# A hand-written schedule of an attention and expert kernel: when two rounding DMAs, a negation and a copy are issued

## The chip, the cores and the metric

The kernel runs on one core of a Trainium2 chip. The metric is device time in microseconds of one execution; the median of three runs of the kernel before is 603.72 us (603.69 to 610.67). The core has five engines that take their instructions in order and meet through semaphores: TensorE (PE; PEld is its weight load), VectorE (DVE), ScalarE (ACT), GpSimd (POOL) and SyncE (SP). PE, DVE, ACT and POOL compute; SP, ACT and POOL also issue DMAs.

## The reference

Attention with a decay bias for 8 batches of 8 heads (576 positions, width 64), then an expert layer for 128 chosen tokens of each batch:

```
scores = (1/8) * q @ k.T
cum    = cumsum(max(s, 0))
scores = where(causal, -1e9, scores + min(-(cum_i - cum_j), 0))
attn   = softmax(scores);   x = attn @ v          # 64 heads
top    = the 128 tokens of a batch with the highest x @ w_gate
out    = x;  out[top] += sigmoid(x[top] @ w_gate) * (relu(x[top] @ w1) @ w2)
```

## The kernel before

One head n is worked through in some 25 small operations. PE multiplies numbers that are rounded to a shorter format (float32r). So that no accuracy is lost, k and q are each kept as a rounded value and a remainder, in four tiles: KA and QA (five buffers each, line 134) hold the rounded values and a few extra rows, KB and QB (four buffers each) hold the remainders and second copies of the rounded values. These operations (lines 149 to 171) fill them:

- hk(n), hq(n): POOL issues a DMA of k or q of head n from HBM; the DMA rounds on its way into KA or QA ("ka<-in_qk_dram" and "qa<-in_qk_dram" in the views).
- kn(n): ACT writes the negated rounded k into the lower half of KB. ka(n): POOL issues a DMA that adds the exact k onto it ("kb<-in_qk_dram"); what stays is the remainder. kb(n): ACT copies the rounded k into the upper half of KB. kn and kb look alike in the views: ACT "kb<-ka".
- qn(n): ACT writes the negated rounded q into QB (ACT "qb<-qa"). qa(n): POOL's adding DMA onto it ("qb<-in_qk_dram"). qb(n): SP copies the rounded q into the other half of QB ("qb<-qa").

With them, PE makes the scores twice. s0 to s3 (tiles "s") have queries on the partitions and serve only for each row's maximum, which DVE takes ("mj<-s", "m"). mrows(n) turns the five columns of maxima into rows on PE ("s<-ident,m"), ACT negates them ("mr<-s") and issues a small DMA ("qa<-mr") that puts them into QA as one more row of the product. st0 to st3 (tiles "st") have keys on the partitions, from KA, QA and then KB, QB; ACT takes their exponential ("pt<-st"), POOL zeroes the part above the diagonal ("pt<-pt"), and av0 to av3 multiply with v on PE ("pa<-vt,pt"). DVE divides by the sums ("xt<-pa,z") and SP stores. The tiles s and st share four PSUM buffers (psS, line 126): a new one starts when ACT or DVE has read what stood in its buffer.

Work on the experts' weights, the choice of tokens and the experts' products ("w1hl", "sct", "ph", "py") is cut into small steps, of which one follows in each slot.

The order is written out by hand. START (line 44) lists the first operations one by one. After it, time is cut into slots, eight to a head; an operation at position p in SCHEDULE (line 57) is emitted for head n in slot 8n + p, and within a slot in the list's order (line 780). So for the head n whose st0 is in slot 8n, hk(n) stands 32 slots ahead, four heads earlier. InOrder (line 24) keeps every engine's instructions in this order. Nothing here is a time: a slot lasts as long as the engines need.

Of the kernel before, what the change touches and what calls it, by code (L numbers as in the profile page):

```python
# [23 lines left out]
class InOrder:  # L24
# [18 lines left out]

START = [
# [4 lines left out]
    ("rows", 3), ("fill", 5), ("rows", 2), ("fill", 2), ("kn", 2), ("qn", 2), ("qb", 2),  # L49
# [6 lines left out]
]  # L56
SCHEDULE = [
# [5 lines left out]
]  # L63

# [774 lines left out]
```

## Time and profile before

| | |
|---|---|
| median of three runs | 603.72 us (603.69 to 610.67) |
| the profiled execution | 610.3 us; its span, first to last instruction, 608.6 us |
| PE busy | 537.2 us (88%) |
| DVE, ACT, POOL busy | 326.1 (54%), 295.3 (49%), 301.6 us (50%) |
| mean granted clock of TensorE | 0.909 |
| software DMA queue (POOL's) | 42.55 MB, 36.4% of 16 engines' span |

A row of the timeline gives start, duration, engine and operation, and in brackets the idle time of the engine before it and what ended that. A row of the waits gives who waited for whom, the sum, the number of times and the longest. The granted clock (PEclk) is 1.00 at 2.4 GHz and 0.50 at 1.2 GHz; a value between is a mean over a stretch that has both.

### The profile page before, as it was taken

How to read it: one execution, taken by the hardware profiler on the slowest of the kernel's cores; microseconds unless marked ns; L12 is line 12 of the kernel's file. 1: busy time of each engine (PE TensorE's matmuls, PEld its weight loads, DVE VectorE, ACT ScalarE, POOL GpSimd, SP SyncE). 2: the span in 40 equal slices, each digit the busy share in tenths (PEclk: the TensorE clock that was granted, in tenths of full speed). 3: DMA queues.
4: the chain of work that ended last, by engine and by line, in shares of the span. 5: the costliest groups of instructions: out<-in, count | busy, mean ns of one | idle time of the engine just before them, and what ended most of it. 6: DMA issues, size and time to landing. Idle time of an engine off the chain costs nothing. (4 is left out here: it accounts for less than half of the span.)

```text
span 608.6 us, 11656 instructions
## 1 busy us (share of the span) xinstructions
PE 537.2 (88%) x3843; PEld 491.2 (81%) x3843; DVE 326.1 (54%) x1350; ACT 295.3 (49%) x658; POOL 301.6 (50%) x629
## 2 busy tenths in 40 slices
PE   6978877888988799778999989899898898999996
PEld 2767767788877798678999988899788888999874
DVE  6434435655456647366466646565265635573562
ACT  4545355544555455555564445564354455652121
POOL 8554444446555565465554455444455546433240
PEclk8977789978899959898999979999998869999999
DMA  5856766565676775655656766565566666532200
GB/s 129 193 127 133 164 147 164 109 135 121 149 162 129 174 182 126 158 123 122 132 123 141 158 154 129 114 132 95 132 157 135 135 139 133 129 64 40 89 19 34
DMA packets 54798, 78.04 MB, mean 128 GB/s; under 512 B 7705, under 2 KB 26452, under 8 KB 54738
## 3 DMA queue, kind: packets, MB, share of 16 engines
q0 software_dynamic: 22080, 42.55, 36.4%
q1 hardware_dynamic: 29724, 30.38, 18.8%
q10 hardware_dynamic: 2934, 4.36, 2.3%
q8 instruction: 31, 0.51, 0.3%
q14 instruction: 29, 0.24, 0.1%
HBM read 55.84 MB, written 11.53 MB: 111 GB/s over the span
## 5 line engine op out<-in xcount | busy, mean ns | idle before, releaser
L34 PE MATMUL pa<-vt,pt 128*96 128x95 f32 (+2 forms) x1920 | 248.8, 277 | 3.3 <-POOL pt L34 3.3
L34 PEld LDWEIGHTS pa<-vt,pt 128*96 128x96 f32 (+2 forms) x1920 | 235.8, 193 | 8.3 <-POOL pt L34 4.7
L34 POOL TENSOR_SCALAR_AFFINE_SELECT pt<-pt 128x128 f32<-128x128 f32 (+1 forms) x320 | 119.0, 464 | 244.5 <-ACT pt L34 244.0
L34 DVE CUSTOM_DVE_ANT_0 mj<-s,maskf 128x192 bf16<-128x192 f32 (+4 forms) x320 | 140.5, 470 | 120.7 <-PE s L34 118.9
L34 ACT ACTIVATE pt<-st 128x288 f32<-128x288 f32 (+3 forms) x320 | 124.3, 440 | 89.1 <-PE st L34 65.3
L34 PE MATMUL st<-qa,ka 67*128 67x288 f32 (+9 forms) x384 | 128.8, 344 | 24.5 <-ACT pt L34 16.2
L34 PE MATMUL s<-ka,qa 66*128 66x64 f32 (+4 forms) x384 | 120.3, 374 | 28.5 <-ACT mr L34 22.5
L34 ACT ACTIVATE qb<-qa 64x576 fp32r<-64x576 f32 x64 | 43.7, 683 | 146.8 <-DMA qa<-in_qk_dram 146.7
L34 PE MATMUL st<-qb,kb 128*128 128x288 f32 (+4 forms) x384 | 108.4, 317 | 0.0
L34 PEld LDWEIGHTS st<-qa,ka 67*128 67x128 f32 (+3 forms) x384 | 77.6, 202 | 36.7 <-ACT pt L34 22.9
L34 PEld LDWEIGHTS s<-ka,qa 66*128 66x128 f32 x384 | 73.7, 220 | 36.3 <-ACT mr L34 25.9
L34 ACT ACTIVATE kb<-ka 64x576 fp32r<-64x576 f32 x128 | 86.9, 679 | 7.9 <-DMA ka<-in_qk_dram 4.1
L34 PEld LDWEIGHTS st<-qb,kb 128*128 128x128 f32 (+1 forms) x384 | 77.7, 202 | 1.4
L34 POOL DMA_DIRECT2D kb<-in_qk_dram x64 | 71.3, 1114 | 2.5 <-issue 2.2
L34 POOL DMA_DIRECT2D ka<-in_qk_dram x66 | 54.9, 832 | 3.8 <-DMA ka<-in_qk_dram 1.1
L34 POOL DMA_DIRECT2D qa<-in_qk_dram x66 | 53.7, 813 | 3.5 <-issue 2.0
L34 POOL DMA_DIRECT2D qb<-in_qk_dram x64 | 54.3, 848 | 0.0
L34 DVE CUSTOM_DVE_ANT_0 mj<-s,maskf,md 128x64 bf16<-128x64 f32 x64 | 18.0, 281 | 31.7 <-PE s L34 30.5
L34 DVE TENSOR_TENSOR xt<-pa,z 128x320 f32<-128x320 f32 x64 | 31.1, 486 | 0.1
L34 POOL DMA_INDIRECT out_dram<-xe,idx x8 | 8.6, 1070 | 36.6 <-DVE xe L34 26.7
L34 DVE CUSTOM_DVE_ANT_0 junk<-xt,wg 128x512 bf16<-128x512 f32 (+1 forms) x40 | 26.5, 681 | 0.2
L34 DVE DVE_READ_ACCUMULATOR2_ANT m<- 128x1 f32 x320 | 26.4, 83 | 0.0
(284 smaller groups left out, 517.8 us busy)
## 6 DMA issues: line engine op xcount, KB each, us to landing
vt<-in_v_dram SPq DMA_DIRECT2D x32, 325.0 KB
ka<-in_qk_dram POOLq DMA_DIRECT2D x66, 144.0 KB, 3.7
qa<-in_qk_dram POOLq DMA_DIRECT2D x66, 144.0 KB, 4.2
qb<-qa SPq DMA_DIRECT2D x64, 144.0 KB
kb<-in_qk_dram POOLq DMA_DIRECT2D x64, 144.0 KB, 4.4
qb<-in_qk_dram POOLq DMA_DIRECT2D x64, 144.0 KB, 3.4
out_dram<-xt SPq DMA_DIRECT2D x32, 192.0 KB
wr<-in_w_dram ACTq DMA_DIRECT2D x16, 256.0 KB
```

The source lines that it names most:

```text
L34: return self._tc.keep_in_program_order(call(*args, **kwargs))
```

## The change

Six entries of SCHEDULE get other positions, two entries of the list trade places within their slot (kb and qn), and START gets another order. hk moves from 32 to 34 slots ahead of its head's slot 8n and hq from 30 to 33; qn from 26 to 18, kb from 18 to 10, qa from 15 to 11, and qb from 19 to 21. No operation is added or removed, and no buffer changes. In START, hq of head 2 and hk, hq of head 4 move ahead, v of heads 2 and 4 is loaded later, and the fills (matmuls on zeros) between them are dealt out in another way.

```diff
 START = [
     ("vload", 0), ("rows", 0), ("s0", 0), ("s1", 0), ("fill", 2), ("kn", 0), ("qn", 0), ("qb", 0),
-    ("hk", 2), ("ka", 0), ("qa", 0), ("kb", 0), ("s2", 0), ("s3", 0), ("hq", 2), ("kn", 1), ("qn", 1), ("qb", 1),
+    ("hk", 2), ("hq", 2), ("ka", 0), ("qa", 0), ("kb", 0), ("s2", 0), ("s3", 0), ("kn", 1), ("qn", 1), ("qb", 1),
     ("fill", 5), ("kb", 1), ("ka", 1), ("qa", 1), ("rows", 1), ("s0", 1),
-    ("vload", 2), ("hk", 3), ("hq", 3), ("s1", 1), ("mrows", 0), ("s2", 1), ("s3", 1),
+    ("hk", 3), ("hq", 3), ("hk", 4), ("hq", 4), ("s1", 1), ("mrows", 0), ("s2", 1), ("s3", 1),
...
 SCHEDULE = [
-    ("norm2", 16), ("av0", 10), ("s2", -14), ("side", 0), ("norm0", 15), ("hk", -32),
-    ("kb", -18), ("av2", 13), ("kn", -21), ("qb", -19), ("hq", -30), ("ka", -13),
+    ("norm2", 16), ("av0", 10), ("s2", -14), ("side", 0), ("norm0", 15), ("hk", -34),
+    ("qn", -18), ("av2", 13), ("kn", -21), ("qb", -21), ("hq", -33), ("ka", -13),
...
```

On ACT the place is the end of a head's work, between the exponentials of st2 and st3 of head 9 and those of st0 and st1 of head 10. Before (the first "kb<-ka" is kn(12), the second kb(12); "qb<-qa" is qn(13); w1hl is a copy of weights):

```order
L34 ACTIVATE kb_87<-ka_86 64x576
L34 ACTIVATE pt9_1097<-st9_2_1134 128x288
L34 ACTIVATE pt9_1097<-st9_3_1139 128x288
L34 ACTIVATE pt9_1097<-st9_3_1139 96x96
L34 ACTIVATE w1hl_147<-wr6_1057 128x512
L34 ACTIVATE kb_87<-ka_86 64x576
L34 ACTIVATE qb_89<-qa_88 64x576
L34 ACTIVATE mr11_1188<-s11_3_1130 5x128
L34 DMA qa_88<-mr11_1188 1x5x128
L34 ACTIVATE pt10_1195<-st10_0_1196 128x448
```

The same place with the change, from the exponential of st2 on ("qb<-qa" is now qn(12), and "kb<-ka" behind it kb(11)):

```order
L34 ACTIVATE pt9_1095<-st9_2_1131 128x288
L34 ACTIVATE pt9_1095<-st9_3_1136 128x288
L34 ACTIVATE pt9_1095<-st9_3_1136 96x96
L34 ACTIVATE w1hl_147<-wr6_1054 128x512
L34 ACTIVATE qb_89<-qa_88 64x576
L34 ACTIVATE kb_87<-ka_86 64x576
L34 ACTIVATE mr11_1187<-s11_3_1127 5x128
L34 DMA qa_88<-mr11_1187 1x5x128
L34 ACTIVATE pt10_1193<-st10_0_1194 128x448
```

The two operations have changed places, and both now serve one head earlier in the row of heads than they did: the negation stays in the same place of the period and takes the q of another head.

On POOL, head 8's zeroing and the four DMAs of its period, before ("qb" is qa(10), "qa" hq(12), "kb" ka(10), the last "ka" hk(13)):

```order
L34 AFFINE_SELECT pt8_1005<-pt8_1005 128x128 x3
L34 DMA qb_89<-in_qk_dram 64x576
L34 DMA qa_88<-in_qk_dram 64x576
L34 DMA kb_87<-in_qk_dram 64x576
L34 AFFINE_SELECT pt8_1005<-pt8_1005 128x128
L34 AFFINE_SELECT pt8_1005<-pt8_1005 96x96
L34 DMA ka_86<-in_qk_dram 64x576
L34 AFFINE_SELECT pt9_1097<-pt9_1097 128x128 x3
```

And with the change ("kb" is ka(10), "qb" qa(10), "ka" and "qa" hk(13) and hq(13)):

```order
L34 AFFINE_SELECT pt8_1003<-pt8_1003 128x128 x3
L34 DMA kb_87<-in_qk_dram 64x576
L34 AFFINE_SELECT pt8_1003<-pt8_1003 128x128
L34 AFFINE_SELECT pt8_1003<-pt8_1003 96x96
L34 DMA qb_89<-in_qk_dram 64x576
L34 DMA ka_86<-in_qk_dram 64x576
L34 DMA qa_88<-in_qk_dram 64x576
L34 AFFINE_SELECT pt9_1095<-pt9_1095 128x128 x3
```

One DMA instead of three now stands between the two groups of zeroing of a head, and three behind the second; hq is of one head later.

On PE, in head 8, the scores of head 10, with what each waits for; before:

```order
L34 MATMUL pa1_151<-vt6_614,pt7_916 128x95 [waits Pool_49]
L34 MATMUL pa1_151<-vt6_614,pt7_916 128x95 x2
L34 MATMUL s10_2_1023<-ka_86,qa_88 128x512 [waits DVE_49]
L34 MATMUL pa1_151<-vt6_614,pt7_916 128x95 x3
L34 MATMUL s10_3_1035<-ka_86,qa_88 128x64 [waits Activation_49]
L34 MATMUL st8_2_1039<-qa_88,ka_86 128x288 [waits DVE_49]
```

And with the change:

```order
L34 MATMUL pa1_151<-vt6_611,pt7_914 128x95 [waits Pool_49]
L34 MATMUL pa1_151<-vt6_611,pt7_914 128x95 x2
L34 MATMUL s10_2_1020<-ka_86,qa_88 128x512 [waits Activation_49]
L34 MATMUL pa1_151<-vt6_611,pt7_914 128x95 x3
L34 MATMUL s10_3_1032<-ka_86,qa_88 128x64 [waits DVE_49]
L34 MATMUL st8_2_1036<-qa_88,ka_86 128x288 [waits Activation_49]
```

The order of PE's work is the same, but the four PSUM buffers are dealt out in another way: the buffer in which head 9's maxima were turned, which ACT must read as mr(9), goes to s2 of head 10 instead of s3, one group of av matmuls sooner.

## Rows read from the trace of the kernel before

**Rows 1.** Page, part 1: busy us, share of the span, instructions

```profile
PE 537.2 (88%) x3843; PEld 491.2 (81%) x3843; DVE 326.1 (54%) x1350; ACT 295.3 (49%) x658; POOL 301.6 (50%) x629
```

**Rows 2.** Waits of PE over the whole span: us in total, times, longest

```profile
PE s L34 <- ACT mr L34: 22.5, 19, 2.5
PE st L34 <- ACT pt L34: 16.2, 25, 1.1
...
PE st L34 <- DMA qa<-in_qk_dram: 3.8, 1, 3.8
```

**Rows 3.** Waits of ACT over the whole span

```profile
ACT qb L34 <- DMA qa<-in_qk_dram: 146.7, 56, 6.0
```

**Rows 4.** Stretches by stage: length, busy of each engine, clock, DMA share, GB/s

```profile
core 0: us, PE busy (x) PEld busy (x) DVE busy (x) ACT busy (x) POOL busy (x), PEclk, DMA share, GB/s
...
45.25:287.44 242.19, 203.70 (x1434) 188.83 (x1432) 129.97 (x545) 124.06 (x278) 126.75 (x264) 0.87 0.64 143
287.44:346.64 59.20, 59.20 (x475) 56.45 (x474) 35.11 (x153) 31.63 (x73) 29.97 (x63) 1.00 0.63 139
346.64:370.21 23.57, 21.74 (x163) 20.71 (x162) 11.89 (x55) 12.51 (x28) 14.05 (x31) 0.86 0.63 141
370.21:434.02 63.81, 60.84 (x493) 57.69 (x492) 37.51 (x164) 33.25 (x76) 28.77 (x62) 1.00 0.58 127
434.02:508.56 74.54, 65.69 (x468) 61.23 (x467) 38.20 (x169) 37.11 (x84) 39.48 (x87) 0.86 0.63 134
508.56:566.00 57.44, 55.63 (x443) 53.31 (x442) 33.60 (x140) 26.28 (x63) 21.69 (x49) 0.97 0.45 95
```

**Rows 5.** ACT's groups from 45.25 to 287.44: busy, mean ns, idle before

```profile
L34 ACT ACTIVATE mr<-s 5x128 fp32r<-5x128 f32 x28 | 7.0, 251 | 0.7 <-PE s L34 0.7
```

**Rows 6.** Timeline of all engines from 465.9 to 482.2

```profile
465.98 0.79 POOL L34 DMA_DIRECT2D qa<-in_qk_dram  x1
...
470.33 0.68 ACT L34 ACTIVATE qb<-qa 64x576 fp32r<-64x576 f32 x1 [3.59 <-DMA qa<-in_qk_dram]
...
471.22 0.30 PE L34 MATMUL s<-ka,qa 66*128 66x64 f32 x1 [1.40 <-ACT mr L34]
...
472.02 1.03 ACT L34 ACTIVATE pt<-st 128x448 f32<-128x448 f32 x2 [0.85 <-PE st L34]
...
472.62 0.40 PE L34 MATMUL st<-qa,ka 67*128 67x288 f32 x1 [0.75 <-ACT pt L34]
...
473.12 0.54 POOL L34 TENSOR_SCALAR_AFFINE_SELECT pt<-pt 128x128 f32<-128x128 f32 x2 [0.19 <-ACT pt L34]
...
474.15 0.80 POOL L34 DMA_DIRECT2D qa<-in_qk_dram  x1
...
474.37 1.80 PE L34 MATMUL pa<-vt,pt 128*96 128x95 f32 x10
...
482.15 1.01 PE L34 MATMUL pa<-vt,pt 128*96 128x95 f32 x10
```

**Rows 7.** Stretches as in Rows 4: head 49, head 52, part of head 52

```profile
445.45:450.96 5.51, 5.51 (x52) 5.42 (x51) 5.41 (x22) 3.78 (x9) 4.04 (x11) 1.00 0.87 233
467.09:476.51 9.42, 7.27 (x52) 6.75 (x51) 5.37 (x25) 3.96 (x9) 5.21 (x13) 0.86 0.52 98
474.00:477.00 3.00, 3.00 (x17) 2.95 (x17) 1.45 (x7) 1.19 (x4) 2.78 (x6) 0.50 0.57 91
```

**Rows 8.** Timeline of all engines in head 49

```profile
445.73 0.27 ACT L34 ACTIVATE mr<-s 5x128 fp32r<-5x128 f32 x1
...
447.05 0.47 PE L34 MATMUL s<-ka,qa 66*128 66x512 f32 x1
...
449.46 0.68 ACT L34 ACTIVATE kb<-ka 64x576 fp32r<-64x576 f32 x1
```

**Rows 9.** Tile qb: issue to landing of its DMAs

```profile
DMA to landing us min/median/max: 3.0/3.4/7.0
```

**Rows 10.** Timeline of POOL, 13 to 14: two of eight DMA issues in a row

```profile
13.21 1.83 POOL L34 DMA_DIRECT2D qb<-in_qk_dram  x1
...
13.73 1.86 POOL L34 DMA_DIRECT2D ka<-in_qk_dram  x1
```

**Rows 11.** POOL's groups from 45.25 to 287.44, columns as in Rows 5

```profile
L34 POOL TENSOR_SCALAR_AFFINE_SELECT pt<-pt 128x128 f32<-128x128 f32 (+1 forms) x142 | 58.6, 534 | 108.5 <-ACT pt L34 108.2
```

More of the change, by code (lines that the diff above doesn't have):

```diff
@@ L45 @@
     ("vload", 0), ("rows", 0), ("s0", 0), ("s1", 0), ("fill", 2), ("kn", 0), ("qn", 0), ("qb", 0),
[1 row of a table removed]
[1 row of a table added]
     ("fill", 5), ("kb", 1), ("ka", 1), ("qa", 1), ("rows", 1), ("s0", 1),
[1 row of a table removed]
-    ("rows", 3), ("fill", 5), ("rows", 2), ("fill", 2), ("kn", 2), ("qn", 2), ("qb", 2),
[1 row of a table added]
+    ("rows", 2), ("rows", 3), ("vload", 2), ("fill", 7), ("kn", 2), ("qn", 2), ("qb", 2),
     ("st0", 0), ("st1", 0), ("ka", 2), ("qa", 2), ("st2", 0), ("st3", 0),
[2 rows of a table removed]
[2 rows of a table added]
     ("ka", 3), ("qa", 3), ("fill", 5), ("av2", 0), ("st0", 1),
     ("st1", 1), ("fill", 4), ("mrows", 2), ("s0", 3), ("s1", 3), ("s2", 3), ("kb", 3),
[1 row of a table removed]
+    ("rows", 4), ("vload", 4), ("fill", 1), ("av3", 0), ("s3", 3),
 ]
 SCHEDULE = [
[4 rows of a table removed]
[4 rows of a table added]
     ("st3", 4), ("mrows", -9),
```

9 rows, old and new, of tables (SCHEDULE, START) are left out of this document.

## The prediction

> **What bounds the kernel now.** PE is busy for 88% of the span [rows 1], but that is a mean over two kinds of stages. I first cut the span by what PE does. While experts' products run (287.44 to 346.64), PE has no idle time at all and its clock is granted at 1.00 [rows 4]; nothing that other engines do sooner can shorten this. In the 28 heads from 45.25 to 287.44 (28 "mr", one per head [rows 5]) PE is idle for 242.19 - 203.70 = 38.5 us, and the clock's mean is 0.87. The stretches from 346.64 and from 434.02 look alike [rows 4]. The question is thus what these plain heads wait for.
>
> PE's waits answer: for ACT, which has not yet read the turned maxima (22.5 us) or taken an exponential (16.2 us) [rows 2]. And ACT waits for one thing above all: 146.7 us in 56 waits before the negation qn, until the rounding DMA of q, hq, has landed [rows 3]. ACT runs in order, so mr, its small DMA and the exponentials stand behind qn, though they need nothing of it.
>
> The timeline shows that this closes a loop [rows 6]. POOL issues hq at 465.98. ACT's qn starts at 470.33, 4.35 us later, after 3.59 us of idling. Then come qn, mr and mr's DMA issue, so that the next exponential starts only at 472.02, 1.69 us later. POOL zeroes at 473.12 and only then reaches the next hq, at 474.15 (2.13 us). The sum is 8.17 us, and no head in this loop can be shorter on average. The stages agree: 242.19 / 28 = 8.65 us a head, and 74.54 / 9 = 8.28 us for the nine heads from 434.02.
>
> How long a head is without the wait, one row shows: head 49, in which hq had landed early, takes 5.51 us with PE never idle and the clock at 1.00 [rows 7].
>
> The clock is the second cost. In head 52 PE idles 9.42 - 7.27 = 2.15 us, 1.40 of it before a score and 0.75 before an st product; behind these waits the clock is 0.50 (1.2 GHz) from 474 to 477 [rows 6, 7]. The same ten av matmuls take 1.80 us there and 1.01 us at 482.15, where it is back: a factor of 1.78 [rows 6].
>
> **The change part by part.** *hq, hk and qn.* hq moves from 4 slots ahead of qn to 15 (33 - 18), about 15/8 of a head. Even in a head of 5.51 us that is 10.3 us, against the 4.35 us in the loop; the longest landing of the like DMA into qb is 7.0 us [rows 9]. So qn starts without a wait and the loop is cut. hk to kn becomes 13 slots instead of 11, 9.0 us at 5.51 us a head. I cost both at nothing; if their cover were gone, the old wait of up to 3.59 us would return.
>
> *What was queued behind qn.* mr and the exponentials start as soon as PE is done. ACT's own work is 124.06 / 28 = 4.43 us a head, weight copies included, plus about 0.85 us while mr's DMA is issued and ACT stands still [rows 4, 6]: 5.28 us, just below the 5.51 us of PE. Heads with weight copies will hold PE up a little.
>
> *kb and qa later.* kb still has 10 slots until st, qa 11: 7.6 us at 5.51 us a head, against 3.4 us of landing and 7.0 at worst [rows 9]. Hidden by the product of one and a half heads; a whole wait would cost PE a few microseconds now and then, not in each head. qb on SP goes 2 slots sooner and feeds nobody sooner than qa does.
>
> *POOL's order.* Two DMAs leave the place between a head's two groups of zeroing and go behind the second, where POOL idled 108.5 us in the stage until the next exponential [rows 11]. av gets its data sooner. On the new order hk stands behind zeroing that has itself waited for the last product of the buffer, so no wait for the buffer is added.
>
> *The PSUM buffers.* s2 instead of s3 now waits for mr. In head 49 mr runs from 445.73 for 0.27 us and s2 starts at 447.05: 1.05 us to spare [rows 8]. Also ACT's last copy ended there at 450.14, 0.82 us before the head's end; with qn in that place, 0.68 us long, it still fits, by 0.1 us. This is the tightest spot, so I keep some idle time in the sum.
>
> *START.* hk and hq of head 4 are issued in a gap of POOL; the wait of 3.8 us in which PE stands until a q lands [rows 2] belongs to DMAs whose place in POOL's row stays. I take 0, with 1 us lost and 5 us gained (the wait, and the clock after it) as bounds.
>
> *The sum.* The granted share gives the time at half clock: a mean of 0.87 means 26% of the stretch. Work there lasts 1.78 times as long, so 0.44 of that time is lost.
> - 45.25 to 287.44: idle 38.5 us; half clock 0.26 x 242.19 = 63.0 us, lost 27.6. Together 66.1; I keep back a tenth of the idle, 4 us, for the tight spot: **62**.
> - 346.64 to 370.21: idle 1.8, half clock 6.6 us, lost 2.9: **4.7**.
> - 434.02 to 508.56: idle 8.9, half clock 20.9 us, lost 9.1; less 1: **17**.
> - 370.21 to 434.02 and 508.56 to 566: idle 3.0 and 1.8, clock 1.5; two thirds of it, since some waits are of the experts' own: **4**.
>
> That is 87.7 us, and a span of 608.6 - 87.7 = 520.9 us; with the 1.7 us around the span, 522.6 us against the profiled execution's 610.3. This one lies at the top of the three runs; from the median, 603.72, the same gain leads to 516.0. I take the middle, **519 us**. A cross-sum: 203.70 - 27.6 = 176 us of work at full clock in 28 heads is 6.3 us a head, and head 49, with no expert step, has 5.5.
>
> A rule of the Trainium skill speaks against so much. Perfetto Trace Analysis, Identifying the Most-Contended Engine, says that a kernel gets faster by way of its busiest engine, and no instruction of PE is removed here. Taken alone, it would leave PE's 537.2 us and allow no more than its idle time to go. The rows differ: PE's busy time is itself stretched by the clock [rows 6, 7]. What remains of the rule is the rival of the clock, below.
>
> **The rivals.** *The clock does not come back.* If half clock had another cause than the idle time, only idle time would go: 38.5 + 1.8 + 8.9 + 4.8 - 5 = 49 us, 555 us from the median. For it: PE runs smaller products here than in the experts' stage. Against it: head 49, a plain head, at 1.00 [rows 7].
>
> *Transfers crowd.* The DMA share of 0.64 over 242.19 us is 5.5 us of all sixteen engines per head [rows 4], so at 6 us a head they would be over 90% busy. If they could be filled only to 0.8, a head would take 6.9 us: 28 x (6.9 - 6.4) + 9 x 0.7 = 20 us less gain, some 540 us. Against it: head 49 ran at a share of 0.87 and 233 GB/s [rows 7]. The page DMA: Bandwidth & Descriptors, Issuing engines are not separate DMA queues, holds that DMAs of all engines interleave on the same sixteen; by it an earlier issue brings no bandwidth, and 5.5 us would be the floor. In head 49 the trace agrees that there is little above.
>
> *Slower: POOL becomes the bound.* POOL's issues come in runs of three now. In a run of eight an issue is shown with up to 1.86 us [rows 10]; four of these and 58.6 / 28 = 2.1 us of zeroing [rows 11] are 9.5 us a head, more than 8.65. It decides from 1.64 us per issue on, and would give 28 x 0.9 + 9 x 1.2 = 36 us more, 640 us. Against it: even in that run the next issue starts 0.52 us later [rows 10].
>
> *No change.* If s2's wait for mr or DVE took the place of qn's in every head, the heads would stay at 8.2 us or more: 600 us. Against it: 1.05 us to spare, and DVE busy for 129.97 of 242.19 us [rows 4, 8].
>
> **How the numbers follow.** The forecast has 0.70, crowding 0.10, the clock 0.10, no change 0.05, slower 0.05. About 2% is what a measurement of this kernel can tell from no change. Faster by more: 0.70 + 0.10 + 0.10 = 0.90; same 0.05; slower 0.05. The range goes from 502 (everything idle and all lost clock gone, 66.1 + 4.7 + 18 + 6.3, and START's 5: 100 us, rounded down) up past crowding to 552; outside it are the last three cases, 0.20.
>
> **What would show it.** In the changed profile ACT's wait before qb should be under 15 us; POOL's issue of hq should come some 10 us ahead of qn; heads without expert work should take 5.5 to 6.7 us, with PEclk at 0.97 or more from 45 us to the experts' stage; the experts' heads should keep their length of about 8.4 us (59.20 us for seven [rows 4]). The prediction is wrong if ACT's wait stays above 50 us, if PE's wait for mr grows instead of shrinking from 22.5 us, or if landings rise beyond 8 us.

## The result

| | kernel before | with the change |
|---|---|---|
| median, same chip | 606.43 us (603.69 to 610.67) | **512.83 us** (511.57 to 516.56) |
| profiled execution, span | 608.6 us | 509.9 us (time 511.64) |
| ratio | | **0.846**, interval 0.838 to 0.854 |

The kernel is 15.4% faster. The forecast was 519 us in a range of 502 to 552. The span fell by 98.7 us; the sum had 87.7. In what follows a ratio's interval is of 95%, and the comparisons leave out executions that lie 1.5% or more above the fastest of their kernel, so that a ratio and a quotient of medians can differ a little.

Two rows of the changed kernel's page, engines and granted clock in 40 slices (compare [rows 1]):

```profile
PE 485.2 (95%) x3841; PEld 452.6 (89%) x3843; DVE 324.8 (64%) x1350; ACT 297.1 (58%) x658; POOL 303.6 (60%) x629
...
PEclk8889997999999999699999999999999999999999
```

PE does the same work in 52 us less of busy time. What is left of waiting stands in the waits of ACT and of PE (us in total, times, longest), the answers to [rows 2, 3]:

```profile
ACT pt L34 <- PE st L34: 86.0, 82, 4.7
ACT mr L34 <- PE s L34: 34.9, 41, 2.4
...
PE s L34 <- DVE ka L34: 4.8, 1, 4.8
PE st L34 <- DMA qa<-mr: 3.6, 4, 1.3
PE st L34 <- DMA qa<-in_qk_dram: 3.5, 1, 3.5
PE st L34 <- DVE m L34: 2.5, 3, 1.9
```

The row of 146.7 us in which ACT waited for q has gone; the roles are turned round, and ACT now waits for PE's products. PE's waits for mr (22.5 us) and for the exponentials (16.2 us) have gone too. One group of ACT's instructions, with its idle time at the end of the row, says the same of the negation itself:

```profile
L34 ACT ACTIVATE qb<-qa 64x576 fp32r<-64x576 f32 x64 | 43.2, 675 | 2.4 <-issue 1.3 <-POOL pt L34 0.6 <-DVE idx L34 0.4
```

The stages of [rows 4], cut at the same heads, with the start ahead of them (length, busy of PE, PEld, DVE, ACT, POOL, clock, DMA share, GB/s); the last row is one plain head, 53. (A packet's whole time is counted in the stretch in which it starts, so that the DMA share of a short stretch can pass 1.)

```profile
0.00:44.87 44.87, 34.46 (x184) 24.25 (x187) 22.03 (x81) 21.82 (x38) 30.91 (x68) 0.85 0.69 156
44.87:223.13 178.26, 171.07 (x1433) 164.98 (x1432) 129.15 (x545) 125.58 (x278) 125.98 (x262) 0.95 0.88 193
223.13:282.34 59.21, 59.21 (x475) 56.47 (x474) 35.16 (x153) 31.86 (x74) 29.64 (x64) 1.00 0.65 141
282.34:300.33 17.99, 17.89 (x164) 17.35 (x162) 11.78 (x55) 12.77 (x29) 15.20 (x33) 1.00 0.79 181
300.33:360.41 60.08, 60.08 (x493) 57.63 (x492) 37.37 (x164) 32.96 (x77) 31.43 (x66) 1.00 0.66 141
360.41:413.70 53.29, 53.29 (x468) 51.74 (x467) 38.46 (x170) 37.49 (x84) 38.03 (x84) 1.00 0.83 180
413.70:467.28 53.58, 53.58 (x443) 51.60 (x442) 33.24 (x139) 26.59 (x64) 22.13 (x49) 1.00 0.48 101
390.45:395.98 5.53, 5.53 (x52) 5.43 (x51) 5.09 (x24) 4.07 (x9) 4.06 (x10) 1.00 1.05 242
```

From 223 us on PE has next to no idle time, at full clock. The table sets the gains against the terms of the sum.

| heads | before, us | after, us | gain | forecast |
|---|---|---|---|---|
| start, to head 3 | 45.25 | 44.87 | 0.4 | 0 |
| 3 to 30 | 242.19 | 178.26 | 63.9 | 62 |
| 31 to 37, experts | 59.20 | 59.21 | 0 | 0 |
| 38 to 40 | 23.57 | 17.99 | 5.6 | 4.7 |
| 48 to 56 | 74.54 | 53.29 | 21.3 | 17 |
| 41 to 47 and 57 to 63 | 121.25 | 113.66 | 7.6 | 4 |

The distance of hq from qn can be read in the timeline of POOL and ACT. The q that POOL issues at 384.89 is negated at 394.47:

```profile
384.89 0.84 POOL L34 DMA_DIRECT2D qa<-in_qk_dram  x1
...
388.94 0.67 ACT L34 ACTIVATE qb<-qa 64x576 fp32r<-64x576 f32 x1
...
394.47 0.67 ACT L34 ACTIVATE qb<-qa 64x576 fp32r<-64x576 f32 x1
```

That is 9.58 us, where it was 4.35 [rows 6]; the negation at 388.94 takes the q of the head before, and neither of the two has idle time ahead of it.

### The profile page after: what moved, and what is told of

Its sections match the earlier page's. It is cut to its first block, busy times and chain, and to the rows that moved or that the text cites. A ratio compares the mean times of both kernels' runs of the same rounds, so it can differ in the third digit from the quotient of the medians.

```text
span 509.9 us, 11696 instructions
## 1 busy us (share of the span) xinstructions
PE 485.2 (95%) x3841; PEld 452.6 (89%) x3843; DVE 324.8 (64%) x1350; ACT 297.1 (58%) x658; POOL 303.6 (60%) x629
## 5 line engine op out<-in xcount | busy, mean ns | idle before, releaser
L34 PE MATMUL pa<-vt,pt 128*96 128x95 f32 (+2 forms) x1920 | 229.3, 262 | 0.8 <-POOL pt L34 0.8
L34 PEld LDWEIGHTS pa<-vt,pt 128*96 128x96 f32 (+2 forms) x1920 | 216.6, 179 | 4.5 <-POOL pt L34 1.2
L34 POOL TENSOR_SCALAR_AFFINE_SELECT pt<-pt 128x128 f32<-128x128 f32 (+1 forms) x320 | 105.8, 379 | 148.9 <-ACT pt L34 147.4
L34 PE MATMUL st<-qa,ka 67*128 67x288 f32 (+9 forms) x384 | 119.4, 322 | 9.9 <-DMA qa<-mr 3.6
L34 PE MATMUL s<-ka,qa 66*128 66x64 f32 (+4 forms) x384 | 110.9, 347 | 4.8 <-DVE ka L34 4.8
L34 PE MATMUL st<-qb,kb 128*128 128x288 f32 (+4 forms) x384 | 102.9, 305 | 0.1
L34 PEld LDWEIGHTS s<-ka,qa 66*128 66x128 f32 x384 | 66.8, 199 | 8.6 <-POOL qa L34 5.4
L34 POOL DMA_DIRECT2D qb<-in_qk_dram x64 | 59.2, 928 | 2.6 <-issue 2.6
L34 POOL DMA_DIRECT2D kb<-in_qk_dram x64 | 56.9, 890 | 3.9 <-issue 2.6
L34 ACT ACTIVATE mr<-s 5x128 fp32r<-5x128 f32 x63 | 16.7, 265 | 35.9 <-PE s L34 34.9
```

The lines of the kernel that those rows point to most:

```text
L34: return self._tc.keep_in_program_order(call(*args, **kwargs))
```

## The experiments

Two theories stood against each other from the start. **The loop**: hq, its landing, qn, mr, the exponential, zeroing and the next hq follow one another, so a head can't be shorter than their sum. **The clock**: the short waits throw PE to half speed, and that lost speed is most of the cost. Then there is the question which of the change's seven parts (six moved entries and START) does the work. All edits are to the tables unless said otherwise.

### qn alone

```diff
- ("qn", -26)
+ ("qn", -18)
```

> The kernel before, with the negation alone moved: qn from 26 to 18 slots ahead; everything else stays. Loop theory (the time before is set by the chain q's DMA issue, landing, qn, mr, exponential, zeroing, next issue): hq is now 12 slots ahead of qn, 8.3 us in a head of 5.51 us, more than the longest landing of 7.0 us, so the chain is cut and nearly all the gain comes: 510 to 525 us, ACT's wait before qb below 20 us. Rival (the new order on POOL, with hk and hq behind both zeroings, or the sooner issue is needed): 560 us or more, with the wait partly there.

Measured: 510.80 us, ratio 0.841 (0.836 to 0.846). One number in one table brings the whole gain. The same group of ACT as above:

```profile
L34 ACT ACTIVATE qb<-qa 64x576 fp32r<-64x576 f32 x64 | 43.1, 674 | 2.8 <-DMA qa<-in_qk_dram 2.7
```

2.7 us of waiting for q are left of 146.7, although hq is issued in its old place. The negation had to come later; the transfer didn't have to come sooner.

### Everything but qn

```diff
- ("qn", -18)
+ ("qn", -26)
```

(in the changed kernel, so that hq is 7 slots ahead of qn)

> The changed kernel with qn back at 26 slots ahead; hk, hq, qb, kb, qa and START as changed. Loop theory: hq is 7 slots ahead of qn, 4.8 us in a head of 5.51 us, about its landing of 4.4 to 5.2 us, and hq's issue no longer hangs on the exponential that stands behind the same head's qn but on one a head earlier, so the chain spans two heads: 5.7 to 6.5 us a plain head, 525 to 550 us, ACT's wait before qb 20 to 80 us. Rival (only the later negation counts, the DMAs sent sooner bring nothing): above 590 us.

Measured: 532.77 us, ratio 0.878 (0.873 to 0.883). ACT still waits:

```profile
ACT qb L34 <- DMA qa<-in_qk_dram: 41.4, 22, 3.8
```

So moving qn later and moving hq sooner are two ways to open the same loop, and with hq alone 7 slots are not quite enough: landings of q have a median of 5.2 us here and reach 8.2.

### hq alone, two slots sooner and two slots later

```diff
- ("hq", -30)
+ ("hq", -32)     and, in the second kernel, ("hq", -28)
```

> The kernel before, with q's rounding DMA alone two slots sooner (hq from 30 to 32 slots ahead), which puts it in front of the first zeroing of a head on POOL. Loop theory: its issue no longer waits for the exponential that stands behind qn, so the chain spans two heads, 6 to 6.8 us a plain head: 530 to 560 us. Rival (two slots, some 2 us, are simply taken off a wait of 2.6 us a head, and the rest of 0.6 us a head stays, or the landing takes longer as transfers crowd): 580 us or more.

> The kernel before, with hq alone two slots later (28 slots ahead), which on POOL puts it behind one more DMA issue (ka), 0.54 us from start to start, and in front of the second zeroing. Loop theory: the chain is longer by this issue and by nothing else, so each of some 40 plain heads takes 0.5 us more: 20 us more than before, about 627 us. Rival (the plain heads are set by the transfers or by PE at half clock, and the wait before qn only fills what they leave): within 5 us of before.

Measured: 520.03 us (ratio 0.852, 0.845 to 0.860) and 653.37 us (1.077, 1.072 to 1.081). Both go in the loop's direction; both sizes were missed, the gain and the loss being larger than I wrote. ACT's wait in the two kernels:

```profile
ACT qb L34 <- DMA qa<-in_qk_dram: 32.5, 20, 3.2
```

```profile
ACT qb L34 <- DMA qa<-in_qk_dram: 221.7, 60, 6.1
```

The later hq shows the loop best. Its timeline, POOL and ACT over one turn:

```profile
484.51 1.11 POOL L34 DMA_DIRECT2D qa<-in_qk_dram  x1
...
489.27 0.68 ACT L34 ACTIVATE qb<-qa 64x576 fp32r<-64x576 f32 x1 [4.79 <-DMA qa<-in_qk_dram]
...
490.94 1.03 ACT L34 ACTIVATE pt<-st 128x448 f32<-128x448 f32 x2 [0.83 <-PE s L34]
...
493.60 1.15 POOL L34 DMA_DIRECT2D qa<-in_qk_dram  x1
```

The parts are 4.76 + 1.67 + 2.66 = 9.09 us, against 4.35 + 1.69 + 2.13 = 8.17 before [rows 6]. hq now stands third in POOL's row (0.53 us more until its issue) and lands 0.41 us later. The expectation had the first of these and not the second: the turn grew by 0.92 us instead of 0.5. The 40 plain heads (3 to 30, 38 to 40, 48 to 56) take 378.65 us in this profile against 340.30 before, 0.96 us more each, and that is 38 of the 44 us by which the span grew. A smaller part was missed too: the loop, at 9.09 us, is also longer than the experts' heads (8.46 us on average [rows 4]), which it had left alone so far. The same seven heads, columns as above:

```profile
310.68:375.30 64.62, 60.64 (x476) 56.72 (x474) 35.44 (x153) 31.11 (x74) 30.86 (x64) 1.00 0.57 125
```

64.62 us instead of 59.20, with PE idle for 4 us where it had none. In the other direction, hq two slots sooner, the two slots take hq in front of the zeroing it had followed; one q issued at 385.16 is negated at 390.51 there. ACT waits in 20 heads instead of 56, and for 3.2 us at most.

### The clock without the loop's being opened

```diff
- fill=[0, 2, 0, 0]
+ fill=[0, 2, 0, 0] + [2] * 26 + [0] * 18 + [2] * 8
```

This is the kernel before, with more matmuls on zeros on PE in the plain heads (list entries 4 to 29 and 48 to 55 get two per odd slot).

> The kernel before with two more groups of matmuls on zeros per head on PE in the heads without expert work, so that PE is idle for less of the time; no DMA, qn or wait is moved. It tells the loop from the clock. Theory (the loop hq - qn - exponential - zeroing - hq bounds a head at some 8.2 us, and the lost clock only rides along): ACT's wait for the q landing stays at 120 to 160 us, PEclk rises towards 1 in these heads, and the time is 590 to 610 us. Rival (the lost clock is the larger part of the cause): with the clock back, heads drop to 7.3 us or less and the time is 570 us or lower.

Measured: 608.03 us, ratio 1.001 (0.997 to 1.004). ACT's wait, then heads 8 to 30 together and head 8 by itself:

```profile
ACT qb L34 <- DMA qa<-in_qk_dram: 153.5, 55, 4.9
```

```profile
90.67:285.39 194.72, 176.52 (x1342) 149.56 (x1363) 109.06 (x463) 100.68 (x227) 105.31 (x214) 1.00 0.63 140
...
90.67:97.90 7.23, 7.23 (x60) 6.24 (x59) 3.90 (x16) 4.64 (x10) 3.96 (x9) 1.00 0.43 82
```

The clock is whole, yet a head takes 194.72 / 23 = 8.47 us, while a head with fills in which PE never stands can take 7.23 (head 8), so the fills themselves are not what holds it at 8.47. One turn of the loop there (hq at 178.69, qn at 182.96, exponential at 184.95, hq at 187.19) is 8.50 us. The lost clock had cost the kernel before nothing by itself: it filled time in which PE would otherwise have waited longer. The clock theory falls, and with it a plan to mend this kernel with fills while the loop is closed.

### The start, and kb and qa

```diff
  START of the kernel before in the changed kernel           (first)
- ("kb", -10), ("qa", -11)
+ ("kb", -18), ("qa", -15)                                   (second)
```

> The changed kernel with the order of the first stages (START) of the kernel before; the moves in the loop's table stay. The prediction put this part at 0, between 1 us lost and 5 us gained by the new order. Theory: the stand of 3.5 us of head 1 for a q is there with either order, so the time is that of the changed kernel within 3 us, 509 to 516 us. Rival: if fetching heads 3 and 4 ahead of the masks was worth something, the old order is 3 to 6 us slower, 515 to 518 us.

> The changed kernel with kb back at slot -18 and qa back at -15; qn, hq, hk and the start stay as changed. The prediction costed the later kb and qa at nothing. Theory: both were hidden before and are hidden now, so 510 to 516 us, with waits for kb and qa before st no larger than now (3.6 us in all). Rival 1: the later places cost waits (the one of 1.3 us in head 8 and its half clock among them): 505 to 509 us. Rival 2: kb ahead of zeroing keeps POOL from av's data and heads grow by 0.1 us each: 515 to 519 us.

Measured: 514.00 us (ratio 0.846, 0.843 to 0.850) and 515.54 us (0.848, 0.843 to 0.852), against 0.846 (0.838 to 0.854) with all moves. Neither can be told from the changed kernel. The zeros in the sum stand.

### What stood behind the start's wait

The first stages issue hk and hq of heads 0 and 1; the loop issues them a second time, with the same data. That makes the 66 DMAs "qa<-in_qk_dram" for 64 heads.

```diff
-    done = set()
+    done = {("hk", 0), ("hq", 0), ("hk", 1), ("hq", 1)}
```

> The changed kernel, but the loop doesn't issue hk and hq of heads 0 and 1 a second time (their first issues stand in the first stages and the data are the same), so four DMAs fewer. Theory: the 3.5 us in which the st product of head 1 waits for a q landing, and the stretch of half clock behind it (33.2 to 40 us, 6.8 us, of which 0.44 is lost, 3 us), both hang on the second issue: gain about 6 us, 505 to 508 us. Rival: that stretch at half clock is caused by the idle time of the first stages as a whole and q would be late anyway: 510 to 514 us, no gain.

Measured: 502.02 us, ratio 0.821 (0.817 to 0.825), some 11 us less by the medians and more than expected. Head 1 in the changed kernel, and without the second issue:

```profile
26.30:38.84 12.54, 9.00 (x50) 6.68 (x49) 3.75 (x19) 4.26 (x9) 7.54 (x20) 0.77 0.66 152
```

```profile
26.68:33.70 7.02, 6.97 (x50) 5.49 (x49) 3.48 (x17) 4.25 (x9) 5.18 (x15) 1.00 0.74 175
```

5.5 us are gained in this one head: 3.5 of waiting, the rest clock. PE's wait for "qa<-in_qk_dram" is gone from its list; in the changed kernel, and so most likely in the kernel before [rows 2], it hung on a DMA that nobody needed. Most of the rest lies in head 29, which takes 8.35 us instead of 12.84, since no half clock follows its wait in this execution; that part can't be put down to the edit.

### GpSimd beside VectorE

In heads 28 and 29 of the changed kernel PE waits for DVE (1.88 us at the longest) and runs at half clock from 203.8 us on, for 10.2 us. The timeline of DVE and POOL there:

```profile
199.02 2.42 POOL L34 TENSOR_TENSOR w2hl<-wr,w2hl 128x512 fp32r<-128x512 f32 x1
...
199.11 2.75 DVE L34 SCALAR_TENSOR_TENSOR ahead<-row,sc,earlier 128x384 bf16<-128x384 f32 x1
...
202.00 2.00 DVE L34 SCALAR_TENSOR_TENSOR ahead<-row,sc,later 128x320 bf16<-128x320 f32 x1
```

```diff
- wpool=[0, 1, 2, 6, 7]
+ wpool=[]              (with the edit of the run before)
```

> The changed kernel without the second issue of heads 0 and 1 (as in the run before that left it out, 502.0 us), and with all five column groups of w2hl's subtraction on VectorE instead of GpSimd. In the changed kernel, at head 28, VectorE's op ahead<-row,sc,earlier takes 2.75 us and later<-... 2.0 us while GpSimd subtracts w2hl at the same time, and a score waits 2.5 us for VectorE, with half clock behind it. Theory: the two engines hold each other up there; with the subtraction on VectorE those ops take under 1 us, the wait goes and the half clock of 10 us with it, 494 to 500 us. Rival: those ops are slow for another reason, or VectorE's added subtractions, which run on one engine then, come due too late: 501 to 508 us.

Measured: 498.81 us, ratio 0.826 (0.821 to 0.830). The same instructions with the subtraction on DVE:

```profile
192.40 0.69 DVE L34 TENSOR_TENSOR w2hl<-wr,w2hl 128x512 fp32r<-128x512 f32 x1
...
193.01 0.61 DVE L34 SCALAR_TENSOR_TENSOR ahead<-row,sc,earlier 128x384 bf16<-128x384 f32 x1
...
193.75 0.55 DVE L34 SCALAR_TENSOR_TENSOR ahead<-row,sc,later 128x320 bf16<-128x320 f32 x1
```

2.75 us become 0.61 and 2.00 become 0.55, so VectorE had been held up. GpSimd had been too, as far as its spans, which are rough, can tell: where none of these operations runs beside it, its subtraction takes 1.28 to 1.88 us (five in the kernel with the fills, one of them below), against 2.42 here and 3.01 for the one after it. On VectorE it takes 0.69.

```profile
188.26 1.87 POOL L34 TENSOR_TENSOR w2hl<-wr,w2hl 128x512 fp32r<-128x512 f32 x1
```

The Trainium skill, GPSIMD Engine Reference, Specifications, says that GpSimd shares its way to SBUF with VectorE and lists VectorE's instructions with two SBUF inputs among those that contend; the rows of both engines agree.

On the whole time the run settles nothing: its interval overlaps that of the run before, in which the half clock in head 29 happened to be absent too. The profiles lean one way. Heads 28 and 29 together take 12.0 to 13.3 us in the three kernels with the subtraction on VectorE. Of the seven with it on GpSimd and the loop open, in full or in part, four take 18.3 to 22.1 us there and three 13.1 to 13.9.

### The weight loads off ACT's queue

```diff
-                act.dma_start(wr, w[c * P : ...])
+                sp.dma_start(wr, w[c * P : ...])      (with the two edits before)
```

> As the kernel with the subtraction on VectorE, but the weight loads wr are issued by SP instead of ACT, so that the small DMA of mr no longer stands behind them on ACT's queue. In the changed kernel four st products wait 3.6 us in all for that DMA, and half clock of 6.8 us follows at 77.5 us. Theory: the small DMA lands late because of the two loads issued 2 us before it on the same queue: the waits for qa<-mr go below 1 us in all and the time falls by 3 to 6 us against the kernel it is based on. Rival 1: it is late because the transfers are near full there, on whatever queue: no difference (within 2 us). Rival 2: SP issues wr behind its own waits, so that the copies of the weights on ACT wait and the experts start late: slower by 3 us or more.

Measured: 494.91 us, ratio 0.817 (0.814 to 0.821), the fastest kernel of the study. PE's wait for the small DMA of mr, without and with this edit:

```profile
PE st L34 <- DMA qa<-mr: 5.6, 5, 2.0
```

```profile
PE st L34 <- DMA qa<-mr: 2.6, 5, 1.1
```

The time falls by 3.9 us by the medians, and the two intervals just fail to touch (0.8213 and 0.8209), so the edit is probably worth something. The wait halves; I had written "below 1 us". Without the edit 5.4 of the 5.6 us stand in heads 6, 8, 10 and 22, in each of which the two loads went out on ACT's queue 2 to 2.7 us ahead of the small DMA that the head needs; with it heads 8 and 10 are nearly free of the wait, and heads 6 and 22 keep 1.3 us. That speaks for the loads. That the queue alone makes the DMA late is not shown, and two kernels speak against it: with qn alone moved (the first experiment, and the next) the loads stand on ACT's queue in the same way, and PE's list has no wait for this DMA at all. So something in the other moves has to be there too. Crowding (the DMA share is 0.91 in these heads) may be it, but no run shows it.

### qn alone, with the two leftovers mended

The leftovers are the second issue and the subtraction on GpSimd; the weight loads stay on ACT's queue.

```diff
- ("qn", -26)
+ ("qn", -18)     (in the kernel before, with the edits of done and wpool above)
```

> The kernel before with qn alone moved to slot -18, no second issue of heads 0 and 1, and the subtraction of w2hl on VectorE. It tells whether the other moves of the change (hq, hk, kb, qa, the start) are worth anything once the two leftovers are gone. Theory: nothing, so within 3 us of the changed kernel with the same two edits. Rival: the other moves were masked by the leftovers' noise: 4 us or more apart, either way.

Measured: 498.72 us, ratio 0.822 (0.818 to 0.825), against 498.81 with all moves. Beside qn, the moves of the change are worth nothing that can be measured here, and nothing is hidden under the leftovers.

## Why the prediction was right, point by point

**The loop.** It was read off one turn of the timeline, and five runs bear it out: ACT's wait and the time move together from 2.7 us of waiting (510.8 us) over 32.5 (520.0) and 41.4 (532.8) to 221.7 (653.4), and with 153.5 us of it a kernel at full clock is no faster than before.

**The clock.** Here the prediction had the mechanism in part wrong. It called the clock "the second cost". The run with fills shows that it was no cost of its own: as long as the loop was closed, giving the clock back gained nothing. Adding the idle time and the lost clock still gave about the right sum, since with the loop open a head takes what PE's own work takes at full clock, and the two terms together are what the loop had put on top of that.

**hq, hk and qn.** I wrote 10.3 us of lead; it is 9.58. It covers every landing (at most 7.7 us). What I did not see is that the move of qn alone would do. I counted the lead of all the moves together and not what each gives by itself: qn alone makes it 12 slots, which leave 2.7 us of waiting.

**kb, qa, START, POOL's order, the PSUM buffers: costed at nothing.** The runs that undo START and that undo kb and qa agree, and so does qn alone, which has none of these moves. s2's wait for mr, the tight spot, does not appear among PE's waits.

**The plain heads.** I expected 5.5 to 6.7 us; 24 of the heads 3 to 29 lie between 5.51 and 6.63. Three don't: 7 (7.12 us), 8 (8.57) and 29 (12.84). I expected PEclk at 0.97 or more from 45 us to the experts; it is 0.95, since two short waits (1.35 us for the small DMA of mr, 1.88 us for DVE) each go with a stretch at half clock.

**The experts' heads.** Unchanged: 59.21 us against 59.20.

**Crowding.** It costs little: head 53 takes 5.53 us at 242 GB/s. But the DMAs into qa do land later, with a median of 5.2 us instead of 4.2 and 7.7 at most; the lead of 9.58 us took that up.

**POOL as the bound.** Its issues come 0.52 to 0.55 us apart (384.37 and 384.89 are two of a run of three), and POOL goes on waiting for the exponentials. It did not become the bound.

**The busiest engine.** The rule of the Trainium skill (Perfetto Trace Analysis, Identifying the Most-Contended Engine), taken alone, left PE its 537.2 us. They fell to 485.2, and to 474.8 in the fastest kernel, with no product removed, so part of the busy time had been no work. The same section of the Trainium skill says that the busy share of matmuls is not a good measure of how near TensorE is to its limit. The rows agree with that; the prediction had left it out. The rival that was left of the rule, the clock that does not come back, is out: the mean granted clock rose from 0.909 to 0.968.

**Where the sum was off.** It was 11 us short. 3.6 of them are the waits that I put down to the experts' own: I took two thirds of their idle and clock, 4 us, and 7.6 came, more than the whole of it, 6.3. 4.3 are heads 48 to 56: I kept back 1 us of idle that went too, and PE's busy time for the same 468 products fell from 65.69 to 53.29 us, by 12.4, where I had 9.1 for the clock. 2.8 are the other plain heads, and 0.4 the start. What I had mostly left out is thus busy time that was neither work nor half clock. In heads 3 to 30 it is hidden by what the leftovers still cost, so that the near hit there, 62 us against 63.9, is in part luck. The same 28 heads in the fastest kernel, all at full clock:

```profile
39.00:206.59 167.59, 162.96 (x1434) 157.24 (x1432) 126.53 (x550) 125.02 (x277) 119.98 (x256) 1.00 0.91 205
```

PE's busy time for the same 1434 products was 203.70 us [rows 4], so 40.7 us of it were no work. I had 27.6, all of them clock. That part was about right: the stretches at half clock held 63.1 busy us and 324 products, which at the mean of all 1434 would take 324 x 162.96 / 1434 = 36.8 us here, so an estimate of 26.3 us was lost to the clock. The other 14 us of busy time went in stretches at full clock. My reading is that a product that starts after a wait has none ahead of it to overlap with: at full clock st<-qa,ka of 67x288 lasts nearly as long in either kernel (379 and 341 ns on average), but adds 304 ns to PE's busy time before and 178 ns in the fastest kernel. So waiting costs more than the view of the waits books as idle. The ends of matmuls are modelled in the profile, so this last step is read, not shown by a run.

## What to carry to other kernels

Where an in-order engine waits for a DMA in each turn, follow the turn until it comes back to that DMA's issue; if it does, the sum of its parts is about the length of a turn (8.17 us here, heads of 8.5 on average), and moving either end (the consumer later or the issue sooner) opens it. How much comes depends on whether the lead then covers the landing: 12 slots did but for 2.7 us of waiting, 7 left 41.4. A better clock on an engine that waits in such a loop bought nothing. After the loop is open, look at each single stretch of half clock and at what PE waited for just ahead of it: here the three edits to what was found that way (a DMA issued twice, a subtraction beside VectorE, two loads ahead of a small DMA) took off another 18 us together, by the medians (512.8 to 494.9). Of that, 5.5 us in one head are shown to come from the first; how the rest is shared out is not.

## What was not expected of the hardware

- A VectorE operation of 0.61 us took 2.75 us beside a GpSimd subtraction, which itself took 2.42 us, against 1.28 to 1.88 without such company.
- In the changed kernel a wait of 1.35 us ahead of head 8 was followed by half clock, which made that head 3.05 us longer (8.57 us, granted clock 0.62, PE never idle, against 5.52 in head 12). Yet a wait of 1.99 us ahead of another st product in the kernel with the subtraction on VectorE left the clock at 1.00. What tells the two apart is not settled here.
- Transfers that fill 0.91 of the engines' time, at 205 GB/s over 28 heads, left room for heads of 5.99 us on average (167.59 / 28), and some took 5.51 us, as head 49 did in the kernel before.
